# Token rows gathered one product earlier, and the second matrix's blocks in the order 0, 2, 1, 3, in an attention and mixture-of-experts kernel

## The chip, the cores and the metric

One core of a Trainium2 chip runs the whole kernel. The metric is device time in microseconds, from start to end of one execution. Five engines work side by side, each through its own instructions in order, and wait for each other through semaphores: TensorE (PE, matrix products), VectorE (DVE), ScalarE (ACT), GpSimd (POOL) and SyncE (SP, which here only issues DMA transfers). POOL issues the indirect transfers, which pick or place rows by a list of indices.

## The reference

The input goes through attention (the sum of a downsampled and a local one), a dense gated layer, and then a mixture of experts. Only the last part is touched by the change:

```python
def _moe2_ref(x, w_gate, w_output_gate, w1, w2):
    logits = x @ w_gate                       # x: 2304 x 512, 8 experts
    e_idx = np.argmax(logits, axis=1)
    ...                                       # gate_w and eom: two factors per token
    for e in range(8):
        mask = e_idx == e
        h = np.maximum(x[mask] @ w1[e], 0.0)  # w1[e]: 512 x 1024
        ye = h @ w2[e]                        # w2[e]: 1024 x 512
        out[mask] = gate_w[mask, None] * eom[mask, e, None] * ye
```

Everything is in float32.

## The kernel before, in words

Attention, the dense layer and the routing fill the first 500 us. Then the experts are worked through in eight ranks, sorted by the number of their tokens. Rank r has room for `CAPS[r]` tokens: 352, 336, 320, 304, 288, 288, 272, 384, so each has three blocks of up to 128 tokens (`NBLK[r]` is 3).

Precision: each float32 operand is split into a rounded part (hi) and the remainder (lo), and each product is the sum of three matmuls: hi by hi (L425), hi by lo of the tokens (L426), lo of the weights by hi (L427), one triple for each 128 x 128 piece of weights. A matrix of an expert comes as four blocks of 128 x 1024 floats (512 KB). `ew_load` (L757) has SP load a block into one of four `raw` buffers, and `ew_split` (L771) makes ACT write its hi (L775) and then DVE or POOL its lo (L777), after which the raw buffer is free. Past rank 0, blocks 0 and 2 have their lo from POOL, and blocks 1 and 3 from DVE. The tiles are W0 to W3 (hi) and W4 to W7 (lo) for the first matrix, W8 to W11 and W12 to W15 for the second: the lo of block 2 of the second matrix is W14, that of block 1 is W13.

The loop at L1111 runs over r = 0 to 6. One turn of it is two stages on PE:

- The second product of rank r: for each of four slices of columns (`dc`) `gb_step` (L827) runs 8 triples, f = 0 to 7, of which the triples of f = 2i and 2i + 1 read block i of the second matrix. After slice dc follow `x_prep`, which transposes block dc of the rows of rank r + 1 (L750) and splits them (ACT and DVE, L754), the split of block dc of the first matrix of rank r + 1, and the load of block dc of its second matrix.
- The first product of rank r + 1: for i = 0 to 3 the split of block i of the second matrix, then `ga_pair` (L806), which makes h[2i] and h[2i+1] (8 triples; ACT writes the hi, DVE the lo, both L803), then `o_step` (L857), which transposes a block of the results of rank r; DVE scales it (`orow`, L850) and POOL scatters it to the output (L851). Last comes the load of block i of the first matrix of rank r + 2, into the raw buffer that the split at this i has freed.

At i = 0, behind the split of block 0, stands `x_gather(r + 2)`: three indirect transfers on POOL (L732), one per block of rows, into `xr`, which has four buffers. In turn r = 0, at i = 1, `overflow_tables` puts some 25 small instructions on DVE.

In this loop the order of every engine is the order in which the program is written. `by_width` (L645) puts each group of products into one of three arms by the true number of tokens, so the streamed width is at times below `CAPS[r]`.

Of the kernel before, what the change touches and what calls it, by code (L numbers as in the profile page):

```python
# [22 lines left out]
NT, DM, DF, E = 2304, 512, 1024, 8  # L23
# [12 lines left out]
NBLK = [-(-c // P) for c in CAPS]  # L36
NBM = max(NBLK)
CMAX = max(CAPS)
CUTS = (0, 16, 48)
NEG = -1e30  # L40
OOB = 1.0e6
RING = 2 * G
# [7 lines left out]
def attention_moe_kernel(ctx: ExitStack, tc: tile.TileContext, q, k, vw_in, v4_in, w1, w2, w3, w_out,  # L50
# [15 lines left out]
    def mt(shape, dt, name, tag=None, bufs=None):  # L66
        return main.tile(shape, dt, name=name, tag=tag or name, bufs=bufs)
# [15 lines left out]
    for j in range(4):  # L83
        nc.gpsimd.iota(ci[32 * j:32 * j + 32, 0:32], pattern=[[1, 32]], base=0, channel_multiplier=-1)
    nc.vector.tensor_copy(cj[:, 0:32], ci[:, 0:32])
    nc.vector.tensor_scalar(cj[:, 32:64], cj[:, 0:32], 0.0, NEG, op0=ALU.is_lt, op1=ALU.mult)
    nc.vector.tensor_scalar(cj[:, 64:96], cj[:, 0:32], 6.0, NEG, op0=ALU.is_gt, op1=ALU.mult)
    nc.vector.tensor_tensor(
        mask, cj[:, 32:64].unsqueeze(1).to_broadcast([P, 6, 32]),
        cj[:, 64:96].unsqueeze(1).to_broadcast([P, 6, 32]), op=ALU.add)  # L90
    nc.vector.memset(mask[0:32, 0, 0:3], NEG)
    nc.vector.memset(mask[96:128, 5, 27:32], NEG)
    eps4 = mt([P, 1], F32, "eps4")
# [49 lines left out]
    def w_tile(n, shape):  # L143
        return mt(shape, F32R, f"W{n}")
# [500 lines left out]
    def by_width(r, C, products):  # L645
# [3 lines left out]
        def arm(a, b):  # L649
            if b - a == 1:  # L650
                products(C - CUTS[a])
                return
            m = (a + b) // 2
            with tc.If(rt["n"][r] > C - CUTS[m]) as cond:
                arm(a, m)
            with cond.Else():
                arm(m, b)

        arm(0, len(CUTS))

    def reg_of(r):
        if r not in rt["reg"]:
            rt["reg"][r] = nc.sync.value_load(rt["ei"][0:1, r:r + 1], min_val=0, max_val=E - 1)
        return rt["reg"][r]
# [51 lines left out]
        pe[0] = next((i for i in reversed(nc.cur_bb.bb.instructions) if i.engine == mybir.EngineType.PE), None)  # L716
        return res

    def x_gather(r, half=None):
        C = CAPS[r]  # L720
        d = rt.setdefault("xr", {})
        for b in range(NBLK[r]):
            n = min(P, C - P * b)
            if (r, b) not in d:
                d[r, b] = bp.tile([P, DM], F32, name="xr", tag="xr", bufs=4)
            dst, src = d[r, b][0:n], yd
            if half == 0:
                dst, src = dst[:, 0:DM // 2], yd.rearrange("n (t d) -> (n t) d", t=2)
            elif half == 1:
                dst, src = dst[:, DM // 2:DM], yh  # L730
            idx = rt["g2"][0:n, b:b + 1] if half == 0 else rt["gi"][0:n, r, b:b + 1]
            ins = nc.gpsimd.indirect_dma_start(out=dst, out_offset=None, in_=src,  # L732
                                               in_offset=bass.IndirectOffsetOnAxis(ap=idx, axis=0))
        return ins

    def x_prep(r, b, k0=0, k1=KD):
        C = CAPS[r]
        if r not in xT:
            if r == 0:
                even = [mt([P, KD, CMAX], F32R, "xT", tag=tag) for tag in ("xh", "xl")]  # L740
                xT.update({i: even for i in range(0, E, 2)})
            else:
                odd = mt([P, 2, KD, CMAX], F32R, "xT", tag="wc")
                xT.update({i: (odd[:, 0], odd[:, 1]) for i in range(1, E, 2)})
        n = min(P, C - P * b)
        t = rt["xr"][r, b]
        ps = at_psum()
        pv = ps[:, 0:512].rearrange("p (k n) -> p k n", k=KD)
        for kk in range(k0, k1):
            nc.tensor.transpose(pv[:, kk, 0:n], t[0:n, P * kk:P * kk + P], ident[0:n, 0:n])  # L750
        c = slice(P * b, P * b + n)
        x = pv[:, k0:k1, 0:n]
        hi, lo = xT[r][0][:, k0:k1, c], xT[r][1][:, k0:k1, c]
        return nc.scalar.copy(out=hi, in_=x), nc.vector.tensor_tensor(lo, x, hi.bitcast(F32), op=ALU.subtract)  # L754
# [3 lines left out]
    def ew_load(r, m, i, t=None):  # L758
        reg = reg_of(r)
        if t is None:  # L760
            t = bp.tile([P, 1024], F32, name="raw", tag="raw", bufs=4)
        if m == 0:
            ins = nc.sync.dma_start(out=t,
                              in_=e_w1[bass.ds(reg, 1), P * i:P * i + P, :].rearrange("o p n -> p (o n)"))
        else:
            ins = nc.sync.dma_start(out=t,
                              in_=e_w2[bass.ds(reg, 1), P * i:P * i + P, :].rearrange("o p n -> p (o n)"))
        raws[r, m, i] = t
        return ins

    def ew_split(r, m, i):  # L771
        t = raws.pop((r, m, i))
        hi = w_tile(8 * m + i, [P, 1024])
        lo = w_tile(8 * m + 4 + i, [P, 1024])
        nc.scalar.copy(out=hi, in_=t)  # L775
        eng = nc.vector if i % 2 != (r == 0 and m == 1) or (r == 0 and m == 0) else nc.gpsimd
        ins = eng.tensor_tensor(lo, t, hi.bitcast(F32), op=ALU.subtract)  # L777
        ew[r, m, i] = (hi, lo)
        return ins
# [32 lines left out]
    def ga_pair(r, f0):  # L812
        C = CAPS[r]
        for f in (f0, f0 + 1):
            gp[f] = psb.tile([P, 512], F32, name="g1", tag="g1", bufs=4)

        def products(n):
            hi, lo = ew[r, 0, f0 // 2]
            for f in (f0, f0 + 1):
                for kk in range(KD):  # L820
                    c = slice(256 * kk + P * (f % 2), 256 * kk + P * (f % 2) + P)
                    mm3n(gp[f], n, C, hi[:, c], lo[:, c], xT[r][0][:, kk], xT[r][1][:, kk], kk == 0, kk == KD - 1)

        by_width(r, C, products)
        return [ga_out(r, f) for f in (f0, f0 + 1)]
# [3 lines left out]
    def gb_step(r, dc):  # L829
        C = CAPS[r]  # L830
        if dc == 0:
            if not oT:
                oT["all"] = mt([P, 2, KD, CMAX], F32, "oT", tag="xr")
            oT[r] = oT["all"][:, r % 2]
        ps = ps2.tile([P, 512], F32, name="g2", tag="g2")

        def products(n):
            for f in range(KF):
                hi, lo = ew[r, 1, f // 2]
                c = slice(512 * (f % 2) + P * dc, 512 * (f % 2) + P * dc + P)  # L840
                t = h2[r, f]
                mm3n(ps, n, C, hi[:, c], lo[:, c], t[:, 0], t[:, 1], f == 0, f == KF - 1)

        by_width(r, C, products)
        nc.scalar.copy(out=oT[r][:, dc, 0:C], in_=ps[:, 0:C])
# [11 lines left out]
    def o_step(r, b):  # L857
        n = min(P, CAPS[r] - P * b)
        ps = at_psum()
        for dc in range(KD):  # L860
            nc.tensor.transpose(ps[0:n, P * dc:P * dc + P], oT[r][:, dc, P * b:P * b + n], ident)
        o_out(r, b, ps)

    def gb_rows(r, b):
        ps = ps2.tile([P, 512], F32, name="g2", tag="g2")
        c = slice(P * b, P * b + P)
        for f in range(KF):
            hi, lo = (w[:, 512 * (f % 2):512 * (f % 2) + 512] for w in ew[r, 1, f // 2])
            t = h2[r, f]
            mm3(ps, t[:, 0, c], t[:, 1, c], hi, lo, f == 0, f == KF - 1)  # L870
        o_out(r, b, ps)
# [192 lines left out]
    for i in range(2):  # L1064
        ew_load(0, 0, i)
    ordered(g2_step, NG - 1, 0, 0)
    rows = x_gather(0, 1)
    behind(rows, ew_load(0, 0, 2))
    behind(rows, ew_load(0, 1, 0, early[:, 0]))
# [6 lines left out]
    with tc.issue_after(store.ins):  # L1076
        ew_load(0, 1, 1, early[:, 1])
    rows = x_gather(0, 0)
    behind(rows, ew_load(0, 0, 3))
    last = ordered(x_prep, 0, NBLK[0] - 1, KD // 2, KD)  # L1080
# [31 lines left out]
    with tc.manual_schedule(engines={et.PE, et.DVE, et.Activation, et.Pool, et.SP}):  # L1112
        for r in range(E - 1):
            for dc in range(KD):
                gb_step(r, dc)
                if dc < NBLK[r + 1]:
                    x_prep(r + 1, dc)
                ew_split(r + 1, 0, dc)
                ew_load(r + 1, 1, dc)
            for i in range(4):  # L1120
                ew_split(r + 1, 1, i)
                if i == 0 and r + 2 < E:
                    x_gather(r + 2)
                ga_pair(r + 1, 2 * i)
                if i < NBLK[r]:
                    o_step(r, i)
                if r + 2 < E:
                    ew_load(r + 2, 0, i)
                if (r, i) == (0, 1):
                    overflow_tables()  # L1130
        for b in range(NBLK[E - 1]):
            gb_rows(E - 1, b)
# [62 lines left out]
```

## Time and profile before

| what | value |
|---|---|
| median of 3 runs | 729.62 us (725.38 to 732.04) |
| the profiled execution | 732.17 us |
| its span, first to last instruction | 730.1 us |
| PE busy | 690.3 us, 95% |
| DVE, ACT, POOL busy | 381.6, 286.1, 332.4 us |
| mean granted TensorE clock | 0.983 of full |

The profile is of one execution. Times in it count from the first instruction. A busy PE row overlaps the next: matmuls are pipelined, and their pace is the distance between the starts of two rows. Where an instruction waited, its row ends with a bracket: the idle time of its engine before it, and what ended that. The executions of the loop are read between 500 and 707 us.

### The profile page before, as it was taken

The numbers are of one execution on the slowest core, as the hardware profiler recorded it, in microseconds if no ns is written. First come the engines' busy times: TensorE is split into PE (matmuls) and PEld (weight loads), VectorE is DVE, ScalarE is ACT, GpSimd is POOL, SyncE is SP. The second block draws the span as 40 slices with busy tenths as digits, with TensorE's granted clock in tenths as the row PEclk, the third lists the DMA queues.
The fourth block names the chain that finished last, engine by engine and source line by source line (L and its number), as shares of the span: only waits on it lengthen the run. The fifth ranks groups of instructions, "written<-read, shape, count | busy, mean of one in ns | idle before, by whom it ended". The sixth has DMA issues, their size and how long they took to land.

```text
span 730.1 us, 14874 instructions
## 1 busy us (share of the span) xinstructions
PE 690.3 (95%) x5710; PEld 659.1 (90%) x5711; DVE 381.6 (52%) x887; ACT 286.1 (39%) x664; POOL 332.4 (46%) x339
## 2 busy tenths in 40 slices
PE   5888999998999999999999999989999999989995
PEld 3787988898999999999999999969999999989994
DVE  8898889853645346253242342563545345345340
ACT  3455525562354136135212221234534545545520
POOL 5976468863474047124002020142636466567431
PEclk9999999998999999999999999989999999999999
DMA  8878545363143124111010100455647456566501
GB/s 325 266 252 275 199 137 193 108 196 119 50 136 110 44 73 119 64 41 45 23 44 1 43 1 30 146 194 173 211 127 235 127 191 216 176 208 231 170 31 42
DMA packets 38287, 98.08 MB, mean 134 GB/s; under 512 B 6019, under 2 KB 12931, under 8 KB 38193
## 3 DMA queue, kind: packets, MB, share of 16 engines
q1 hardware_dynamic: 34768, 86.82, 37.5%
q0 software_dynamic: 3424, 9.93, 3.7%
q8 instruction: 68, 1.11, 0.6%
q14 instruction: 27, 0.21, 0.1%
HBM read 84.93 MB, written 12.29 MB: 133 GB/s over the span
## 4 chain that ended last, share of the span: by engine, by line
PE 52%; issue 18%; POOL 16%; DMA 7%; DVE 6%; ACT 1%; SPq 0%; POOLq 0%; DVEq 0%; ACTq 0%
PE g L419 14%; PE g L421 13%; PE g L420 13%; POOL W L777 6%; POOL out_dram L851 3%; POOL xr L732 2%; DMA v<-in_v_dram 2%; PE at L282 2%; DMA vw<-in_vw_dram 1%; PE g L427 1%; PE at L222 1%; PE g L425 1%; DVE cv L140 1%; PE g L426 1%; PE at L278 1%
## 5 line engine op out<-in xcount | busy, mean ns | idle before, releaser
L419 PE MATMUL g<-xh,W 128*128 128x384 f32 x384 | 131.9, 343 | 0.9 <-ACT a L453 0.9
L421 PE MATMUL g<-xh,W 128*128 128x384 f32 x384 | 129.2, 337 | 0.8 <-POOL W L398 0.7
L420 PE MATMUL g<-xl,W 128*128 128x384 f32 x384 | 129.2, 336 | 0.0
L777 POOL TENSOR_TENSOR W<-raw,W 128x1024 fp32r<-128x1024 f32 x29 | 70.3, 2424 | 78.3 <-ACT W L775 78.3
L458 POOL TENSOR_TENSOR h<-a,h 128x384 fp32r<-128x384 f32 x30 | 30.6, 1020 | 101.6 <-ACT h L456 101.6
L419 PEld LDWEIGHTS g<-xh,W 128*128 128x128 f32 x384 | 72.2, 188 | 2.5 <-ACT a L453 1.2
L421 PEld LDWEIGHTS g<-xh,W 128*128 128x128 f32 x384 | 72.1, 188 | 1.9 <-POOL W L398 1.8
L420 PEld LDWEIGHTS g<-xl,W 128*128 128x128 f32 x384 | 72.2, 188 | 0.1
L427 PE MATMUL g<-h,W 128*128 128x320 f32 (+4 forms) x224 | 66.2, 296 | 3.9 <-POOL W L777 3.9
L425 PE MATMUL g<-h,W 128*128 128x320 f32 (+7 forms) x224 | 68.3, 305 | 1.2 <-ACT xT L754 0.8
L419 PE MATMUL g<-wc,h 128*128 128x272 f32 (+1 forms) x240 | 69.3, 290 | 0.0
L420 PE MATMUL g<-wc,h 128*128 128x272 f32 (+1 forms) x240 | 68.9, 289 | 0.0
L425 PE MATMUL g<-xT,W 128*128 128x288 f32 (+5 forms) x224 | 68.8, 307 | 0.0
L421 PE MATMUL g<-wc,h 128*128 128x272 f32 (+1 forms) x240 | 68.6, 288 | 0.0
L426 PE MATMUL g<-h,W 128*128 128x320 f32 (+4 forms) x224 | 66.1, 295 | 0.8 <-DVE h L803 0.8
L427 PE MATMUL g<-xT,W 128*128 128x320 f32 (+4 forms) x224 | 66.4, 296 | 0.0
L426 PE MATMUL g<-xT,W 128*128 128x320 f32 (+4 forms) x224 | 66.3, 296 | 0.0
L775 ACT CAST W<-raw 128x1024 fp32r<-128x1024 f32 x61 | 63.2, 1048 | 5.5 <-DMA raw<-in_moe_w_dram 5.5
L777 DVE TENSOR_TENSOR W<-raw,W 128x1024 fp32r<-128x1024 f32 x32 | 41.4, 1294 | 38.0 <-ACT W L775 33.2
L454 DVE TENSOR_TENSOR a<-g,a 128x384 f32<-128x384 f32 x48 | 26.6, 554 | 55.0 <-PE g L421 47.0
L803 DVE SCALAR_TENSOR_TENSOR h<-g,h 128x288 fp32r<-128x288 f32 (+6 forms) x64 | 30.5, 486 | 31.0 <-ACT h L803 20.2
L803 ACT ACTIVATE h<-g 128x288 fp32r<-128x288 f32 (+6 forms) x64 | 27.4, 436 | 48.6 <-PE g L427 37.4
(266 smaller groups left out, 1746.6 us busy)
## 6 DMA issues: line engine op xcount, KB each, us to landing
raw<-in_moe_w_dram SPq DMA_DIRECT2D x61, 512.0 KB
f64w<-in_moe_w_dram SPq DMA_DIRECT2D x16, 512.0 KB
f<-in_moe_w_dram SPq DMA_DIRECT2D x16, 512.0 KB
vw<-in_vw_dram SPq DMA_DIRECT2D x16, 384.0 KB
kc<-in_k_dram SPq DMA_DIRECT2D x16, 288.0 KB
qT<-in_q_dram SPq DMA_DIRECT2D x16, 288.0 KB
kz<-in_k_dram SPq DMA_DIRECT2D x32, 144.0 KB
v<-in_v_dram SPq DMA_DIRECT2D x16, 288.0 KB
```

The lines of the kernel that those rows point to most:

```text
L419: nc.tensor.matmul(ps, whi, xhi, start=first, stop=False)
L420: nc.tensor.matmul(ps, whi, xlo, start=False, stop=False)
L421: return nc.tensor.matmul(ps, wlo, xhi, start=False, stop=last)
L425: nc.tensor.matmul(ps[:, 0:w], whi, xhi[:, 0:w], start=first, stop=False)
L426: nc.tensor.matmul(ps[:, 0:n], whi, xlo[:, 0:n], start=False, stop=False)
L427: nc.tensor.matmul(ps[:, 0:n], wlo, xhi[:, 0:n], start=False, stop=last)
L454: nc.vector.tensor_tensor(a, pp[1][:, 0:G], a, op=ALU.mult)
L458: eng.tensor_tensor(lo, a, hi.bitcast(F32), op=ALU.subtract)
L775: nc.scalar.copy(out=hi, in_=t)
L777: ins = eng.tensor_tensor(lo, t, hi.bitcast(F32), op=ALU.subtract)
L803: return nc.scalar.activation(out=t[:, 0, 0:C], in_=ps[:, 0:C], func=AF.Relu), nc.vector.scalar_tensor_tensor(t[:, 1, 0:C], ps[:, 0:C], 0. ...
L851: ins = nc.gpsimd.indirect_dma_start(out=out, out_offset=bass.IndirectOffsetOnAxis(ap=rt["si"][0:n, r, b:b + 1], axis=0), in_=t[0:n], in_o ...
```

## The change

The gather is called block by block. The three blocks of the rows of rank r + 2 are now gathered in the second product of rank r, one behind each of the slices 0, 1 and 2, in place of all three in the first product of rank r + 1. The second matrix of rank r + 1 is loaded, and later split, in the order of blocks 0, 2, 1, 3. Which engine makes the lo of a block stays as it was (0 and 2 POOL, 1 and 3 DVE), so the two splits of POOL now come one after the other, and then the two of DVE.

```diff
+W2ORDER = (0, 2, 1, 3)
-    def x_gather(r, half=None):
+    def x_gather(r, half=None, blocks=None):
         C = CAPS[r]
         d = rt.setdefault("xr", {})
-        for b in range(NBLK[r]):
+        for b in range(NBLK[r]) if blocks is None else blocks:
...
                 ew_split(r + 1, 0, dc)
-                ew_load(r + 1, 1, dc)
+                if r + 2 < E and dc < NBLK[r + 2]:
+                    x_gather(r + 2, blocks=(dc,))
+                ew_load(r + 1, 1, W2ORDER[dc])
             for i in range(4):
-                ew_split(r + 1, 1, i)
-                if i == 0 and r + 2 < E:
-                    x_gather(r + 2)
+                ew_split(r + 1, 1, W2ORDER[i])
                 ga_pair(r + 1, 2 * i)
```

The line numbers of the changed kernel are one higher than those before, down to the loop.

On POOL, in turn r = 5, from the split of block 0 of the first matrix to the last scatter. L777 rows are the lo of a block, `xr` rows a gather, `out_0_dram` rows a scatter. Before:

```order
L777 TENSOR_TENSOR W4_10076<-raw_9706,W0_10075 128x1024
L777 TENSOR_TENSOR W6_10254<-raw_9902,W2_10253 128x1024
L777 TENSOR_TENSOR W12_10342<-raw_10079,W8_10341 128x1024
L732 DMA xr_10345<-yd_72,b_gi_5790 128x512
L732 DMA xr_10347<-yd_72,b_gi_5790 128x512
L732 DMA xr_10349<-yd_72,b_gi_5790 128x512
L851 DMA out_0_dram<-orow_10447,b_si_5791 2304x512
L851 DMA out_0_dram<-orow_10554,b_si_5791 2304x512
L777 TENSOR_TENSOR W14_10562<-raw_10257,W10_10561 128x1024
L851 DMA out_0_dram<-orow_10652,b_si_5791 2304x512
```

The same stretch of POOL in the changed kernel:

```order
L778 TENSOR_TENSOR W4_10076<-raw_9706,W0_10075 128x1024
L733 DMA xr_10079<-yd_72,b_gi_5790 128x512
L733 DMA xr_10170<-yd_72,b_gi_5790 128x512
L778 TENSOR_TENSOR W6_10258<-raw_9902,W2_10257 128x1024
L733 DMA xr_10261<-yd_72,b_gi_5790 128x512
L778 TENSOR_TENSOR W12_10348<-raw_10081,W8_10347 128x1024
L852 DMA out_0_dram<-orow_10447,b_si_5791 2304x512
L778 TENSOR_TENSOR W14_10464<-raw_10172,W10_10463 128x1024
L852 DMA out_0_dram<-orow_10554,b_si_5791 2304x512
L852 DMA out_0_dram<-orow_10652,b_si_5791 2304x512
```

The gathers have moved from behind W12 to places behind W4 and W6, and W14 from behind the second scatter to behind the first.

On DVE, in the first product of the same turn: L777 rows are the lo of a block, `h` rows the lo of the hidden values, `orow` rows the scaled results. Before:

```order
L850 TENSOR_SCALAR orow_10447<-tr_10442,b_gv_6014 128x512
L777 TENSOR_TENSOR W13_10464<-raw_10168,W9_10463 128x1024
L803 SCALAR_TENSOR_TENSOR h2_10543<-g1_10467,h2_10543 128x272
L803 SCALAR_TENSOR_TENSOR h3_10546<-g1_10468,h3_10546 128x272
L850 TENSOR_SCALAR orow_10554<-tr_10549,b_gv_6014 128x512
L803 SCALAR_TENSOR_TENSOR h4_10641<-g1_10565,h4_10641 128x272
L803 SCALAR_TENSOR_TENSOR h5_10644<-g1_10566,h5_10644 128x272
L850 TENSOR_SCALAR orow_10652<-tr_10647,b_gv_6014 32x512
L777 TENSOR_TENSOR W15_10660<-raw_10339,W11_10659 128x1024
```

In the changed kernel:

```order
L851 TENSOR_SCALAR orow_10447<-tr_10442,b_gv_6014 128x512
L804 SCALAR_TENSOR_TENSOR h2_10543<-g1_10467,h2_10543 128x272
L804 SCALAR_TENSOR_TENSOR h3_10546<-g1_10468,h3_10546 128x272
L851 TENSOR_SCALAR orow_10554<-tr_10549,b_gv_6014 128x512
L778 TENSOR_TENSOR W13_10562<-raw_10263,W9_10561 128x1024
L804 SCALAR_TENSOR_TENSOR h4_10641<-g1_10565,h4_10641 128x272
L804 SCALAR_TENSOR_TENSOR h5_10644<-g1_10566,h5_10644 128x272
L851 TENSOR_SCALAR orow_10652<-tr_10647,b_gv_6014 32x512
L778 TENSOR_TENSOR W15_10660<-raw_10345,W11_10659 128x1024
```

W13 has moved from ahead of h2 to ahead of h4; the rest of DVE's order stands.

## Rows read from the trace of the kernel before

**Rows 1.** The page: busy time, share of the span and instructions of each engine.

```profile
PE 690.3 (95%) x5710; PEld 659.1 (90%) x5711; DVE 381.6 (52%) x887; ACT 286.1 (39%) x664; POOL 332.4 (46%) x339
```

**Rows 2.** Waits of PE, whole span: us in total, times, longest us.

```profile
PE g L427 <- POOL W L777: 3.9, 3, 1.3
PE g L426 <- DVE h L803: 0.8, 1, 0.8
```

**Rows 3.** Timeline of PE: start us, us, instruction, [idle before <-releaser].

```profile
623.04 0.38 PE L427 MATMUL g<-h,W 128*128 128x240 f32 x1 [1.29 <-POOL W L777]
...
649.23 0.38 PE L427 MATMUL g<-h,W 128*128 128x240 f32 x1 [1.32 <-POOL W L777]
...
673.13 0.30 PE L425 MATMUL g<-h,W 128*128 128x272 f32 x1
...
674.60 0.27 PE L426 MATMUL g<-h,W 128*128 128x224 f32 x1
676.18 0.37 PE L427 MATMUL g<-h,W 128*128 128x224 f32 x1 [1.31 <-POOL W L777]
```

**Rows 4.** Timeline of POOL, turn r = 5.

```profile
659.54 2.40 POOL L777 TENSOR_TENSOR W<-raw,W 128x1024 fp32r<-128x1024 f32 x1 [4.47 <-ACT W L775]
663.58 2.50 POOL L777 TENSOR_TENSOR W<-raw,W 128x1024 fp32r<-128x1024 f32 x1 [1.64 <-ACT W L775]
666.23 1.80 POOL L732 DMA_INDIRECT xr<-yd,b_gi  x1
...
669.61 0.95 POOL L732 DMA_INDIRECT xr<-yd,b_gi  x1 [0.30 <-issue]
670.87 1.02 POOL L851 DMA_INDIRECT out_dram<-orow,b_si  x1 [0.30 <-issue]
672.19 1.54 POOL L851 DMA_INDIRECT out_dram<-orow,b_si  x1 [0.30 <-issue]
673.74 2.39 POOL L777 TENSOR_TENSOR W<-raw,W 128x1024 fp32r<-128x1024 f32 x1
```

**Rows 5.** Timeline of ACT, turn r = 5: the hi of the second and third block split.

```profile
664.21 1.04 ACT L775 CAST W<-raw 128x1024 fp32r<-128x1024 f32 x1
...
667.35 1.04 ACT L775 CAST W<-raw 128x1024 fp32r<-128x1024 f32 x1
```

**Rows 6.** Timeline of DVE, turn r = 5.

```profile
664.71 0.74 DVE L850 TENSOR_SCALAR orow<-tr,b_gv 128x512 f32<-128x512 f32 x1
665.37 1.79 DVE L777 TENSOR_TENSOR W<-raw,W 128x1024 fp32r<-128x1024 f32 x1
...
667.85 0.74 DVE L850 TENSOR_SCALAR orow<-tr,b_gv 128x512 f32<-128x512 f32 x1
...
670.62 0.44 DVE L803 SCALAR_TENSOR_TENSOR h<-g,h 128x272 fp32r<-128x272 f32 x1 [0.91 <-issue]
670.98 0.73 DVE L850 TENSOR_SCALAR orow<-tr,b_gv 32x512 f32<-32x512 f32 x1
671.64 1.20 DVE L777 TENSOR_TENSOR W<-raw,W 128x1024 fp32r<-128x1024 f32 x1
...
674.62 0.44 DVE L803 SCALAR_TENSOR_TENSOR h<-g,h 128x272 fp32r<-128x272 f32 x1 [1.09 <-ACT h L803]
```

**Rows 7.** Timeline of DVE, turn r = 0, in the overflow tables.

```profile
525.43 0.17 DVE L889 TENSOR_SCALAR b_b<-i 128x18 f32<-128x18 f32 x1
...
525.98 3.03 DVE L893 TENSOR_SCALAR b_b<-b_b 128x18 f32<-128x18 f32 x1
```

**Rows 8.** Timeline of POOL, turn r = 0: W14.

```profile
526.53 2.44 POOL L777 TENSOR_TENSOR W<-raw,W 128x1024 fp32r<-128x1024 f32 x1
```

**Rows 9.** Timeline of SP, turn r = 5: the four loads of the second matrix.

```profile
655.10 9.08 SPq L766 DMA_DIRECT2D raw<-in_moe_w_dram  x4
```

**Rows 10.** Two stretches (second, first product), engines' busy us, PEclk, DMA share, GB/s.

```profile
647.00:661.01 14.01, 11.93 (x103) 11.39 (x102) 3.66 (x6) 6.00 (x11) 6.91 (x4) 1.00 0.52 169
661.01:673.13 12.12, 12.12 (x110) 12.08 (x109) 8.62 (x13) 7.79 (x13) 9.11 (x7) 1.00 0.70 228
```

## The prediction

> **What bounds the kernel now.** I read the busy times first. PE is busy for 690.3 of 730.1 us [rows 1], so only what PE waits for counts. Next I read the waits of PE. In the loop over the ranks its largest named wait is for a lo of weights made by POOL: 3.9 us in three waits, 1.3 us the longest [rows 2]. The timeline of PE puts them at 623.04, 649.23 and 676.18, so in the turns r = 3, 4 and 5, of 1.29, 1.32 and 1.31 us, always on the last matmul of a triple of f = 4, which reads the lo of block 2, W14 [rows 3]. The turns before have no such wait; their products are wider and give POOL more time.
>
> The timeline of POOL tells why W14 is late [rows 4]. In turn 5 POOL makes W12 until 666.08, then three gathers from 666.23 to 670.56, two scatters until 673.73, and only then W14, from 673.74 to 676.13. PE had started its triple of f = 4 and would have gone on at 674.71 (the start of the matmul before, 674.60, and a pace of 0.11 us): W14 is 1.42 us late. Its hi was written long before: in turn 5 ACT casts block 2 at 667.35, until 668.39 [rows 5]. So POOL's queue is late, not data.
>
> **What the change does to W14.** It takes about 4.3 us of gathers out of POOL's queue ahead of W14 (666.23 to 670.56 [rows 4]), and one scatter. I lay turn 5 out anew, with PE as it is now. W12 ends at 666.08 as before. The first scatter needs the first `orow`, which DVE ends at 665.45 [rows 6], and takes 1.02 [rows 4]: until 667.1. Block 2 now has the cast that block 1 had, which ends at 665.25 [rows 5]. So W14 runs from 667.1 to 669.5, 5.2 us before PE wants it. What a slow scatter (1.54 [rows 4]) or a late W12 could add does not use that up. The three waits go: **3.92 us**.
>
> **Where the gathers go.** Their six places a turn cost POOL nothing that ends on PE. The first two fall into the 4.47 us in which POOL idles before W6 [rows 4]; at 0.95 and 0.30 us between them they take 2.5, at the stretched 1.80 each 4.2. The third falls between the end of W6 (661.94) and the start of W12 (663.58), 1.64 us: 0.95 fits, 1.80 makes W12 about 0.6 us late, which comes off the 5.2 us of W14. A gather needs a free `xr` buffer; there are four, and each gather stands behind the transposes that free its own. The rows come a stage sooner than now, and no wait for them stands in this loop. Price: 0, and at worst 0.6 us of slack.
>
> The gathers' transfers now share the DMA engines with loads of the second matrix instead of the first. The second product is the emptier stage: 0.52 of the engines at 169 GB/s, against 0.70 at 228 [rows 10]. In turn 5 the four loads begin at 655.10 [rows 9], and the second block must be there at 664.21 [rows 5]: 9.1 us. Two loads are 1.05 MB, 4.6 us at 228 GB/s; three gathers of 128 rows of 2 KB are 0.79 MB, 3.4 us. Even with all gathers ahead of them the loads have 1.1 us left. Estimated cost: 0.
>
> **The new order of blocks.** Loads and splits keep their distance, since both use the same order. The raw buffer that W14 now frees at i = 1 was freed by DVE at 667.16 [rows 6], and is now at 669.5: the load into it is issued 2.3 us later, but its block is cast only in the next second product, over 10 us on. The load that waited for W14 until 676.13 is issued when W13 ends. Cost: 0.
>
> On DVE, W13 leaves the place ahead of h2 and stands ahead of h4. Its cast is now the third one, which ends at 668.39 [rows 5]; the second `orow` ends at 668.59 [rows 6]. There it meets POOL's W14, until 669.5. What such a meeting costs is in the rows: W13 takes 1.79 us from 665.37, of which POOL's W12 covers the part until 666.08, while W15, which meets no split of POOL, takes 1.20 [rows 4, 6]. The excess, 0.59 us, is about the overlap of 0.71. So W13 ends between 669.8 (no hindrance) and 670.7 (it waits for W14). I take 670.7, by that row. Then h4 and h5 (0.44 each) until 671.6, the third `orow` until 672.3, W15 until 673.5, h6 until 674.0. h7 starts as now at 674.62, because ACT's hi sets it, and ends at 675.06 [rows 6]. PE wants these from its start of this product, 673.13 [rows 3], at 0.113 us a matmul (13 of them to 674.60): h6 by the 20th, 675.3; W15 by the 21st, 675.4; h7 by the 23rd, 675.6. The margins are 1.3, 1.9 and 0.5 us. So W13's move costs 0, but the next thing to be late is this chain of DVE.
>
> The Trainium skill, SBUF — State Buffer, section on who interferes with whom, says that a VectorE instruction with two SBUF inputs and a GpSimd instruction that reads SBUF exclude one another, and that the one issued first holds the port to its end. By that rule W13 waits for W14 in full. The trace agrees (1.79 beside 1.20 us [rows 6]). By it the change brings two such instructions closer together; the sum stays at 3.9 us as long as DVE's margins hold, and is the first rival below where they don't.
>
> **Turn r = 0.** PE also waits once for an h of DVE, 0.8 us [rows 2]. There a DVE instruction of the overflow tables takes 3.03 us, where one of the same size takes 0.17 [rows 7]; it ends at 529.01, and POOL's W14 runs from 526.53 to 528.97 [rows 8]. With two gathers' and more work gone ahead of it, W14 will be over before 525.98. That gives DVE back 2.86 us, and W13, which now stands behind the tables, takes 1.2 of it. The chain to h6 is then some 1.6 us earlier, and the wait goes: 0.8 us. Bounds: if the long instruction stays for another reason, W13 makes the chain 1.2 us later and PE waits up to 2.0, a loss of 1.2. I take the gain of 0.8, since both ends of the long instruction fit W14.
>
> **Sum.** 3.92 + 0.8 = 4.7 us. Against the profiled execution, 732.17 us, that is 727.5. The median of the three runs is 729.62, 2.55 below the profiled one; the same 4.7 us below it is 724.9, my forecast: 0.6% faster. A measurement of this kernel tells about 1% (7.3 us) from no change, so this is "within 1%".
>
> **Rivals.**
>
> 1. DVE's chain takes the place of W14: no change. For it speaks the thin margin of h7, 0.5 us. The bound: POOL's second and third scatter (1.0 us each) each go first and hold DVE up as W14 does. W13 then ends at 671.7, the third `orow` at 673.3, W15 at 675.5, h6 at 675.95, h7 at 676.4, and PE waits 0.8 us. In all six turns r = 0 to 5 that is 4.8 us and eats the gain: about 729.7. Against it: before, a scatter that met W15 was itself stretched (1.54 us beside 1.02 [rows 4]), and W15 was not (1.20 [rows 6]). Half of it would give 727.
> 2. Slower: gathers and loads of the second matrix get in each other's way. The point from which it decides is 4.5 us of delay of the second block (9.1 less 4.6); the gathers' own bytes are worth 3.4. If each turn's cast came 2 us late beyond that and ACT, which then holds h2 and h3 back, passed it on to PE in six turns, that is 12 us less 4.7: 737. Against it: the second product leaves nearly half of the DMA time free [rows 10].
> 3. The change doesn't reach PE: W14 is still late, because its scatter in front waits for something else. It would have to wait 5.2 us more than now. The time would stay at 729.6.
> 4. More than I count: an earlier W14 also frees raw buffers and the loads behind them sooner, and PE's small waits elsewhere in these turns go as well. Their whole is some 2 us: 722.5.
>
> **How the numbers follow.** Forecast (3.9 to 4.7 us less) 0.62, rival 1 in part or whole 0.18, rival 2 0.08, rival 3 0.04, rival 4 0.08. The forecast's own range is 722 to 728, as medians of three runs that spread from 725.38 to 732.04 move by about 3 us. To hold 8 in 10 I reach over rival 1 and a part of rival 4, from 720.5 to 731. Faster by over 1% (below 722.3) needs rival 4 or a low set of runs: 0.14. Slower by over 1% (above 736.9) is rival 2: 0.07. Within 1%: 0.79.
>
> **What would show it.** In the profile after: no wait of PE for W L777; W14 in turn 5 over some 5 us before its triple; POOL's gathers behind W4 and W6; W13 of about 2 us where it meets W14; no 3.03 us in the tables. Wrong would be a wait of PE for DVE's h or W in the turns 3 to 5 (rival 1), or ACT's cast of the second or third block waiting for a DMA (rival 2).

## The result, and the profile after

The changed kernel takes 720.36 us (median of 7 runs, 719.58 to 724.86) against 728.89 us before (7 runs, 725.38 to 732.04). The ratio is 0.9904, with a 95% interval from 0.9875 to 0.9934: about 1.0% faster, between 4.8 and 9.1 us. Timed again later beside the kernel before, it was 722.27 against 728.26 us, ratio 0.9898 (0.9852 to 0.9944). So the sign and the forecast of "within 1%" are right, the forecast of 4.7 us is too small (the loop below gave 7.4), and 720.36 lies just below the range. By the two medians alone it is 8.5 us, 1.2%.

In the profile after, PE is busy for 96% of a span of 717.8 us; the row is laid out as [rows 1]:

```profile
PE 686.0 (96%) x5710; PEld 657.0 (92%) x5711; DVE 377.1 (53%) x887; ACT 286.8 (40%) x664; POOL 334.7 (47%) x339
```

The two profiled spans differ by 12.3 us, more than the medians do, so a part of that belongs to single executions. The loop over the ranks can be cut out: it runs from the first matmul of the second product of rank 0 to the first one of rank 7. On the timeline of PE in the changed kernel these are:

```profile
493.38 0.32 PE L426 MATMUL g<-h,W 128*128 128x352 f32 x1
...
674.67 0.35 PE L426 MATMUL g<-xT,W 128*128 128x384 f32 x1
```

That is 181.29 us. In the kernel before, the same two are at 498.72 and 687.40, 188.68 us. The loop gave **7.4 us**; 5.3 us of the difference of the spans lie ahead of it, where both programs are the same. In three executions of the changed kernel the loop took 181.29, 181.31 and 181.31 us, while its start moved from 493.38 to 500.72. The loop is the sharper measure, and all kernels below are compared by it.

One cause of the 5.3 us is to be seen. In the kernel before, PE waited 2.3 us for a transfer of the attention (`vw`, L282) between 165 and 175 us, and the granted clock then fell for some microseconds. By stretch, with the columns of [rows 10], before and after:

```profile
165.00:180.00 15.00, 12.72 (x99) 11.94 (x99) 4.47 (x14) 2.37 (x6) 5.63 (x7) 0.77 0.44 137
```

```profile
165.00:180.00 15.00, 14.89 (x124) 14.06 (x123) 6.20 (x31) 3.06 (x8) 6.09 (x8) 1.00 0.41 130
```

0.77 of full clock against 1.00, and 99 matmuls against 124. Nothing of the change is near, and a third execution of the changed kernel waits there too, 2.1 us at the longest: this belongs to single executions.

Inside the loop, PE has no wait at all after the change. The list of its waits over the whole span (columns as in [rows 2]) has only lines of earlier and of transitional stages; its longest are

```profile
PE g L348 <- POOL qz L159: 5.8, 1, 5.8
PE g L420 <- DVE wc L385: 3.7, 3, 2.9
```

and both rows of [rows 2] are gone. POOL in turn 5 answers to [rows 4]:

```profile
645.70 1.00 POOL L733 DMA_INDIRECT xr<-yd,b_gi  x1 [0.16 <-issue]
647.01 1.31 POOL L733 DMA_INDIRECT xr<-yd,b_gi  x1 [0.30 <-issue]
648.99 2.40 POOL L778 TENSOR_TENSOR W<-raw,W 128x1024 fp32r<-128x1024 f32 x1 [0.68 <-ACT W L776]
651.54 0.96 POOL L733 DMA_INDIRECT xr<-yd,b_gi  x1
653.04 2.51 POOL L778 TENSOR_TENSOR W<-raw,W 128x1024 fp32r<-128x1024 f32 x1 [0.54 <-ACT W L776]
655.69 1.02 POOL L852 DMA_INDIRECT out_dram<-orow,b_si  x1
656.73 2.43 POOL L778 TENSOR_TENSOR W<-raw,W 128x1024 fp32r<-128x1024 f32 x1
```

The gathers fill gaps that POOL had; W6 (648.99) and W12 (653.04) still wait for their cast by ACT, not for a gather. The last row is W14: it ends at 659.16. PE's triple that reads it comes at

```profile
664.17 0.27 PE L428 MATMUL g<-h,W 128*128 128x224 f32 x1
```

so W14 is 5.0 us early where it was 1.42 us late. DVE in the same turn answers to [rows 6]:

```profile
657.96 2.30 DVE L778 TENSOR_TENSOR W<-raw,W 128x1024 fp32r<-128x1024 f32 x1
660.18 0.78 DVE L804 SCALAR_TENSOR_TENSOR h<-g,h 128x272 fp32r<-128x272 f32 x2
660.88 0.73 DVE L851 TENSOR_SCALAR orow<-tr,b_gv 32x512 f32<-32x512 f32 x1
661.54 1.20 DVE L778 TENSOR_TENSOR W<-raw,W 128x1024 fp32r<-128x1024 f32 x1
662.67 0.99 DVE L804 SCALAR_TENSOR_TENSOR h<-g,h 128x272 fp32r<-128x272 f32 x2
```

W13 takes 2.30 us, since it meets W14 (until 659.16, and 1.10 us on). h7 ends at 663.66; PE wants it 22 matmuls of 0.113 us after 662.59, at 665.1.

Where the 7.4 us lie, by the length of the single products (start to start of PE's rows):

| product | before, us | after, us | difference |
|---|---|---|---|
| second of rank 1 (turn 0's wait for h) | 16.67 | 15.54 | 1.13 |
| second of rank 4 (W14) | 13.85 | 12.30 | 1.55 |
| second of rank 5 (W14 and one short wait) | 14.85 | 12.28 | 2.57 |
| second of rank 6 (W14 and one short wait) | 14.27 | 12.08 | 2.19 |
| the other nine | 129.04 | 129.09 | -0.05 |

### The profile page after: what moved, and what is told of

Its sections match the earlier page's. It is cut to its first block, busy times and chain, and to the rows that moved or that the text cites. A ratio compares the mean times of both kernels' runs of the same rounds, so it can differ in the third digit from the quotient of the medians.

```text
span 717.8 us, 14882 instructions
## 1 busy us (share of the span) xinstructions
PE 686.0 (96%) x5710; PEld 657.0 (92%) x5711; DVE 377.1 (53%) x887; ACT 286.8 (40%) x664; POOL 334.7 (47%) x339
## 4 chain that ended last, share of the span: by engine, by line
PE 69%; DVE 9%; POOL 7%; issue 6%; DMA 5%; ACT 2%; SPq 0%; POOLq 0%; DVEq 0%; ACTq 0%
PE g L420 13%; PE g L422 13%; PE g L421 13%; PE g L426 8%; PE g L428 7%; PE g L427 7%; DVE cv L141 2%; DVE cv L140 2%; DVE wf L142 1%; PE tr L751 1%; PE at L283 1%; DMA v<-in_v_dram 1%; DMA kc<-in_k_dram 1%; PE tr L862 1%; POOL out_dram L852 1%
## 5 line engine op out<-in xcount | busy, mean ns | idle before, releaser
L852 POOL DMA_INDIRECT out_dram<-orow,b_si x24 | 33.2, 1384 | 37.5 <-DVE orow L851 36.0
```

Source lines behind the costliest of these rows:

```text
L852: ins = nc.gpsimd.indirect_dma_start(out=out, out_offset=bass.IndirectOffsetOnAxis(ap=rt["si"][0:n, r, b:b + 1], axis=0), in_=t[0:n], in_o ...
```

## The experiments

The loop is cut out as above. "None" means no wait of PE over 0.3 us in it, "without cause" that no semaphore explains the wait.

| kernel | loop, us | waits of PE in the loop |
|---|---|---|
| before, two executions | 188.68, 187.86 | W14 three times, h in turn 0, one or two short ones |
| changed, three executions | 181.29, 181.31, 181.31 | none |
| gathers alone, two executions | 183.72, 183.57 | h in turn 0, one or more short ones |
| order alone | 188.60 | h four times, W13 in turn 0, two of 1.2 without cause |
| changed, late loads | 183.13 | one of 1.2 without cause |
| changed, extra transfers | 187.29 | two without cause, 2.7 and 1.3 |
| the same, one arm | 192.42 (wider products) | none |
| changed, late h6 | 190.78 | h6 three times, by construction |

### The kernel before again

No edit; a second execution.

> The kernel before, looked at in a second execution, to see which of its waits belong to it and which to one execution. In the first profile the loop takes 188.7 us from the start of the second product of rank 0 to the start of the first product of rank 7; the changed kernel takes 181.3. Theory: the three waits for W14 (1.3 us each, turns 3 to 5), the wait for an h of DVE in turn 0 (0.8) and two short waits of PE behind slice 1 of the second products of ranks 5 and 6 (0.76 and 0.46 us) all come again, and the loop takes 188.7 within 0.5. Rival: the two short waits are chance; they are gone or elsewhere, and the loop takes about 187. What lies before the loop may differ by several us.

```profile
PE g L427 <- POOL W L777: 3.9, 3, 1.3
PE g L426 <- DVE h L803: 0.8, 1, 0.8
PE g L425 <- PE tr L750: 0.6, 1, 0.6
```

The list of PE's waits in this execution, from 490 us on. The waits for W14 and for h are the same to a tenth. Of the two short ones, that of rank 5 came again (0.6 in place of 0.76 us), that of rank 6 did not, and the loop is 0.8 us shorter. So the named waits belong to the kernel; the short ones come at like places, and not always. Their releaser is named as ACT in one execution and PE itself in the other, so the name given is not to be relied on.

### The gathers alone, the order alone

The first leaves the order of blocks as it was, the second the gathers:

```diff
-W2ORDER = (0, 2, 1, 3)
+W2ORDER = (0, 1, 2, 3)
```

> Only the gathers are moved; the blocks keep the order 0, 1, 2, 3. Theory (the gathers in POOL's queue made W14 late): W14 stands behind two scatters, and in turn 5 ends at 672 on the scale of the profile before, 2.7 us ahead of PE; the three waits for W14 are gone and the two short ones with them. In turn 0 W14 still meets the overflow tables of DVE, so that a tiny DVE instruction of about 3 us and PE's wait of some 0.8 to 1.1 us stay. Loop 182.4 us, time about 1 us over the changed kernel. Rival (the place behind the second scatter is what made it late): the waits for W14 stay at 2 us or more in sum, loop 186 or more.

```diff
-                if r + 2 < E and dc < NBLK[r + 2]:
-                    x_gather(r + 2, blocks=(dc,))
                 ew_load(r + 1, 1, W2ORDER[dc])
             for i in range(4):
                 ew_split(r + 1, 1, W2ORDER[i])
+                if i == 0 and r + 2 < E:
+                    x_gather(r + 2)
```

> Only the order of the blocks is changed to 0, 2, 1, 3; the gathers stay behind the first split of the second matrix. Theory: W14 then stands behind the gathers and one scatter, and ends at 674.3 in turn 5, 0.4 us ahead of PE, and by 0.6 and 0.7 us in turns 3 and 4: the waits for W14 go, just so. In turn 0 W14 still meets the tables (about 525.3 to 527.7), and W13 now stands behind them, so PE's wait there stays near 1 us. Loop 182.4 to 183.5 us. Rival (only the gathers matter): waits for W14 stay at 2 us or more in sum, loop 185 or more.

Gathers alone: 719.23 us against 727.39, ratio 0.9878 (0.9845 to 0.9910), loop 183.72. Order alone: 726.58 us against the same 727.39, ratio 0.9997 (0.9970 to 1.0024), loop 188.60. **The gathers carry the change; the order alone is worth nothing.**

PE's waits in the loop with the gathers alone:

```profile
PE g L426 <- ACT xT L755: 1.1, 1, 1.1
PE g L427 <- DVE h L804: 0.8, 1, 0.8
```

The waits for W14 are gone, as expected. The loop is 1.3 us longer than expected (182.4), since a short wait of 1.1 us stands in rank 4, where I had expected none. That in turn 0 stays, as expected: there POOL makes W14 from 519.50 to 521.92, and a tiny instruction of the tables on DVE takes 2.92 us, from 519.03 to 521.95.

With the order alone the waits for POOL go too, and that much of the expectation holds, but others take their place:

```profile
PE g L427 <- DVE h L804: 2.0, 4, 1.2
PE g L426 <- ACT xT L755: 1.2, 1, 1.2
PE g L426 <- issue: 1.2, 1, 1.2
PE g L428 <- DVE W L778: 0.9, 1, 0.9
```

This I had not expected, though a part of it is what the prediction held as its first rival. The timelines of POOL and of DVE in turn 5 show how:

```profile
665.08 1.02 POOL L852 DMA_INDIRECT out_dram<-orow,b_si  x1 [0.30 <-issue]
666.11 2.42 POOL L778 TENSOR_TENSOR W<-raw,W 128x1024 fp32r<-128x1024 f32 x1
```

```profile
665.88 3.75 DVE L778 TENSOR_TENSOR W<-raw,W 128x1024 fp32r<-128x1024 f32 x1
669.55 0.78 DVE L804 SCALAR_TENSOR_TENSOR h<-g,h 128x272 fp32r<-128x272 f32 x2
```

W14 is behind the gathers still, and now meets W15, the last split of DVE. W15 takes 3.75 us in place of 1.20 [rows 6]: it begins in POOL's scatter, is held up through all of W14 (until 668.53), and ends 1.10 us later. h6 and h7 are behind it, and PE waits for them, 0.8 us in the turns 3 to 5 together. The Trainium skill, SBUF — State Buffer, section on who interferes with whom, has these two instructions exclude one another for their whole length, the one that is issued first ahead. 3.75 us is 2.42 and 1.20 with a wait behind the scatter, which agrees in length; that W14, which began 0.23 us after W15, went ahead of it does not. The same happens in turn 0, where W14 meets the first of the tables' instructions,

```profile
518.82 3.18 DVE L883 TENSOR_TENSOR b_cm<-b_rank,i 128x64 f32<-128x64 f32 x1
```

and W13, now behind the tables, is late as well: 0.92 us for W13 and 1.17 for h. In the changed kernel W14 runs from 516.60 to 519.00, before the tables begin, and the instruction of 3.03 us [rows 7] is one of 0.18:

```profile
520.91 0.18 DVE L894 TENSOR_SCALAR b_b<-b_b 128x18 f32<-128x18 f32 x1
```

So the order adds to the gathers what turn 0 loses, 1.0 us. Without them it takes away as much as it gives: the 3.9 us of waits for W14 are gone, and by the idle times 0.8 us for h in the turns 3 to 5, 1.3 us in turn 0 (0.92 and 1.17 in place of 0.83) and 1.1 us of short waits (1.17 and 1.16 in place of 0.76 and 0.46) come in their place. The rest is the slower pace of PE behind a wait. The short waits are those of one execution each.

### The short waits: late loads, or after-effects

Before, W14 held back raw buffers, so that two loads of the next first matrix were issued some 3 us into the second product. This kernel does the same with W14 early:

```diff
-                gb_step(r, dc)
+                done = gb_step(r, dc)
...
+                if dc == 0 and r in (5, 6):
+                    for i in (2, 3):
+                        behind(done, ew_load(r + 1, 0, i))
...
-                if r + 2 < E:
+                if r + 2 < E and not (r in (4, 5) and i >= 2):
                     ew_load(r + 2, 0, i)
```

> The changed kernel, but in turns 4 and 5 the loads of blocks 2 and 3 of the first matrix are issued only when slice 0 of the next second product has left PSUM, some 3 us into it, which is when the kernel before issued them; W14 stays early. Theory A (the two short waits of PE behind slice 1 in ranks 5 and 6 come from loads that a late W14 held back): they come again, 0.4 to 1.1 us each, with no wait for W14; loop 182.3 to 183.3. Theory B (they are an after-effect of PE's wait for W14): no wait, loop 181.3 within 0.3.

Neither came. The loop took 183.13 us, as theory A had it, but by one wait in another place, in the first product of rank 5:

```profile
643.15 0.37 PE L426 MATMUL g<-xT,W 128*128 128x288 f32 x1 [1.20 <-DVE orow L851]
```

Late loads of the same two blocks do not bring the waits of ranks 5 and 6 back, so that they alone caused these is not shown. The run did not set up the case of before either, as the packets that bring instructions (below) show: before, the packet of rank 5 started at 652.43, behind late loads issued at 649.20 and 649.77; here it started at 648.43, ahead of the loads (649.40 and 649.97), and in rank 6 at 672.72, ahead of those from 673.77 on. The other question, whether such a wait is the after-effect of PE's own wait, was put by making h6 late:

```diff
+                if i == 3 and r in (3, 4, 5):
+                    pad = mt([P, G], F32, "pad", tag="t2k", bufs=3)
+                    for _ in range(8):
+                        nc.vector.memset(pad, 0.0)
```

> The changed kernel with eight fillings of a scratch tile on DVE (about 3 us) between W15 and h6 in turns 3, 4 and 5, which makes PE wait for h6 there, 1 to 1.6 us each, without holding back any load. Theory B (the short waits behind slice 1 in ranks 5 and 6 are an after-effect of PE's wait a slice earlier): waits of 0.4 to 1.1 us follow there. Theory F: a wait of PE gives its instructions time to come, and none follows beyond the one or two that every arrangement has. Loop 185 to 186 by F, about 187 by B.

The eight fillings took 4.05 us, not 3, and PE waited 2.19, 2.13 and 2.27 us; the list of its waits in the loop has nothing else:

```profile
PE g L427 <- DVE h L804: 6.6, 3, 2.3
```

No wait behind slice 1 followed, so theory B falls. The loop was 190.78 us, longer than either theory said: the waits were larger than meant, and behind the first of them the clock fell.

```profile
619.00:622.00 3.00, 0.81 (x8) 0.62 (x7) 2.38 (x7) 0.00 (x0) 0.00 (x0) 1.00 0.79 300
622.00:624.00 2.00, 2.00 (x12) 2.00 (x13) 0.18 (x1) 0.71 (x2) 0.00 (x0) 0.63 0.02 7
624.00:626.00 2.00, 2.00 (x12) 2.00 (x12) 0.69 (x1) 1.22 (x2) 0.69 (x1) 0.52 0.00 0
626.00:629.00 3.00, 3.00 (x29) 3.00 (x28) 0.41 (x1) 1.43 (x3) 2.70 (x2) 1.00 0.16 26
```

PE waited until 621.88, and in the 4 us after it ran at 0.63 and 0.52 of full clock, near the lower of its two levels (1.2 GHz): 12 matmuls in 2 us, where the stretch at full clock has 29 in 3. That product lost 1.9 us more than the wait itself. Behind the other two waits the clock stayed at 1.00, and the products lost 0.5 and 0.4 us more.

### The short waits: PE's instructions

The queue that brings instructions (q8 on the page) shows single packets, 16 KB each. In eight of the nine of these waits that are longer than 0.4 us, over five kernels, PE went on 2.3 to 2.6 us after the start of a packet; in the ninth, with late loads, after 4.3 us, and there the packet itself was slow (2.5 us). In the changed kernel a packet starts at 641.81 and slice 2 of rank 5, where the kernel before waits, begins at 644.41, 2.6 us later, with no wait. To test whether transfers can bring such waits about, one transfer of 1 MB from memory to memory was put into turns 3 to 6 (its result is not used), once in the changed kernel and once with a single arm for all widths, in which PE skips no instructions:

```diff
+    spare = dram.tile([512, DM], F32, name="spare")
...
+                if dc == 0 and r >= 3:
+                    nc.sync.dma_start(out=spare, in_=yd[0:512])
```

> The changed kernel with one more transfer from memory to memory (1 MB, its result is not used) issued by SP at the start of the second products of ranks 3, 4, 5 and 6. Theory F: waits of PE without a releaser come in most of these four products, 0.5 to 3 us each, while waits for W or h stay below 0.3 us; each ends 2.4 to 3 us after a packet of the instruction queue. Loop 183 to 190. Rival (they have nothing to do with transfers): at most one such wait, loop 181.3 to 182.8.

```diff
-CUTS = (0, 16, 48)
+CUTS = (0,)
```

> The same extra transfers, and the products have one arm only, so that PE runs through its program without skipping two arms of three; the streamed width is then always the full one, and each turn is longer by up to a fifth. Theory F: PE goes through its instructions a third as fast, and the waits without a releaser of the run with the extra transfers are gone or under 0.5 us in sum. Rival (the transfers slow PE's operands or its stores): the waits stay as there.

With three arms PE's waits are in ranks 5 and 6 (on its timeline):

```profile
648.38 0.58 PE L427 MATMUL g<-h,W 128*128 128x288 f32 x1 [2.70 <-issue]
...
676.55 0.27 PE L427 MATMUL g<-h,W 128*128 128x224 f32 x1 [1.31 <-issue]
```

They end 2.5 and 2.3 us after a packet (645.85 and 674.28). They came in two of the four products, where I had expected most. Behind the first the clock fell too, and that product lost 1.8 us more than the wait (columns as in [rows 10]):

```profile
648.40:650.40 2.00, 2.00 (x9) 2.00 (x10) 0.10 (x1) 0.00 (x0) 0.93 (x1) 0.50 0.91 309
```

What held the packet up is to be seen in the share of the 16 DMA engines (last column but one), in the second product of rank 5. First the changed kernel, then the one with the extra transfers:

```profile
638.50:641.50 3.00, 3.00 (x29) 3.00 (x29) 0.52 (x2) 0.70 (x2) 0.46 (x1) 1.00 1.02 417
642.00:644.00 2.00, 2.00 (x20) 2.00 (x20) 0.69 (x1) 1.07 (x2) 0.84 (x1) 1.00 0.00 0
```

```profile
639.50:645.00 5.50, 5.50 (x52) 5.50 (x51) 1.22 (x3) 2.25 (x4) 1.30 (x2) 1.00 1.07 431
646.00:647.50 1.50, 0.00 (x0) 0.00 (x0) 0.92 (x2) 1.24 (x2) 1.35 (x2) 1.00 0.00 0
```

In both the packet starts as the engines run empty of data, 3.6 us into the product in the one (641.81) and 6.6 us in the other (645.85), where PE had stood still since 645.68. In the kernel before, the late loads filled the engines around its packet (652.43):

```profile
650.50:653.00 2.50, 2.50 (x25) 2.50 (x24) 0.69 (x1) 1.93 (x3) 0.30 (x1) 1.00 0.92 318
```

With one arm there is no wait of PE in the loop at all, with the same extra transfers. The instruction queue in the stretch from 600 to 690 us, three arms and then one (packets, MB, share of 16 engines):

```profile
q8 instruction: 17, 0.28, 1.2%
```

```profile
q8 instruction: 6, 0.10, 0.4%
```

So these waits are PE waiting for its next instructions, as far as one execution of each shows: they come with transfers that hold the packet up, and go when PE runs through its program a third as fast. The one arm also makes the products up to 1.9 us longer, which this run cannot take apart from the fewer instructions. The Trainium skill, Runtime: NRT & Kernel Launch, section on instruction fetch, says that a taken branch to instructions that have not been fetched stops the engine until they are; the 2.70 us with the skipped arms and none without them agree with it.

### The changed kernel again, and beside the gathers alone

> The changed kernel in a second execution. Its first profile has no wait of PE in the loop (181.3 us). In the profiles of four other arrangements of the loop PE has one or two waits of 0.6 to 1.5 us that no semaphore explains, at places that differ, each ending about 2.7 us after a packet of the queue that brings instructions. Theory F (these are PE waiting for its next instructions; they come when a packet is held up): the changed kernel can have one too, 0 to 1.5 us in sum; no named wait over 0.3 us; loop 181.3 to 182.8. Rival (the gathers' new place does away with them): none, loop 181.3 within 0.2.

The loop took 181.31 us with no wait over 0.3 us. Then both were timed together, in five rounds:

> Only the gathers moved, timed beside the changed kernel on one chip, to see what the order of the blocks adds. By the two profiles it adds 1.0 us in turn 0 (the overflow tables) and the absence of one wait for instructions of 1.4 us: 2.4 us, 0.3%. Theory: this kernel is 1 to 2.5 us slower than the changed one, and its loop again takes 183.7 us with the wait for an h of DVE in turn 0 (0.8) and the one wait without a releaser in rank 4. Rival (the order adds nothing that lasts): the two are within 0.5 us.

> The changed kernel, timed beside the one with the gathers alone. Theory: loop 181.3 us as in both earlier profiles, no wait of PE over 0.3 us in it, time 1 to 2.5 us below the kernel with the gathers alone. Rival: within 0.5 us of it.

Gathers alone: 721.22 us (ratio 0.9892, 0.9849 to 0.9936), loop 183.57, again with the wait of 0.8 us in turn 0, and with three products in ranks 4 and 5 longer by 0.2, 0.7 and 0.4 us, in place of one by 1.3. Changed: 722.27 us (0.9898, 0.9852 to 0.9944), loop 181.31. By the profiles the order is worth 2.3 us in the loop, of which 1.0 is turn 0 and the rest short waits, which differ between executions; by the measured times the two can't be told apart (the gathers alone are even 1.1 us lower), because what lies ahead of the loop moves by more. The theory's 1 to 2.5 us of the total are not shown.

## Why the prediction was right, and where not

- **What bounds the kernel: right.** PE's waits were all that counted, and they went: of 188.7 us in the loop, 7.4.
- **W14 in POOL's queue: right, to the number.** Predicted 5.2 us ahead of PE in turn 5, measured 5.0. With the gathers alone the waits go, and with the order alone too: the gathers and the second scatter together made W14 late, and taking either from ahead of it is enough. What sets the two halves apart is what else they bring.
- **The size of these waits: a little small.** I took the three idle times, 3.92 us [rows 2]. By the pace of the rows around them each cost 0.15 us more (1.45, 1.48, 1.47, in sum 4.4): the matmul after a wait starts slowly.
- **Gathers at no cost: right.** POOL's W6 and W12 wait for ACT as before, and no cast of ACT in the loop waited for a load. Two slips in the text of it changed nothing: a turn has three places for gathers, not six, and a third gather of 1.80 us with the 0.30 before it would make W12 0.5 us late, not 0.6 (it took 0.96).
- **W13 behind W14: right.** 2.30 us in place of an estimated 2.1 (668.59 to 670.7), and hidden. The margin that I feared, h7's 0.5 us, was 1.4, as ACT's hi came sooner (0.20 us behind the start of PE's product, 1.06 before; what held it up there is not shown).
- **Turn 0: right mechanism, mis-sized.** The tables' long instruction was W14's doing, as it follows W14 through four arrangements (3.03, 2.92, 3.18 and 0.18 us). I took 0.8 us, the product became 1.13 shorter.
- **The step that failed** is the sum, where it left PE's short waits out. Only rival 4 has them, as PE's "small waits elsewhere in these turns", with "some 2 us" for it all and a chance of 0.08. The two in ranks 5 and 6 were 1.10 and 0.63 us by the rows' pace, and all of that went: 7.4 is 4.4, 1.13 and 1.73, plus 0.1 of small change. In the second execution of before they were 0.9. So rival 4 is what happened (its 722.5 is 2.4 us below the forecast, where its words say some 2), with its mechanism only half right: these are waits for instructions, which other transfers hold up. That the early loads did away with them fits the DMA share around the packets, but is argued; the run with late loads did not set the case up.
- **Rival 1** did not happen here. With the order alone its mechanism is there, DVE's chain held up behind W14, but it is small: 0.8 us in the turns 3 to 5, where the bound had 0.8 in each of six turns. That the gain is gone there (188.60 us) is as much turn 0 and the short waits.
- **The median** is 8.5 us lower where the loop gives 6.6 to 7.4. The rest is within the interval (4.8 to 9.1), and the loop starts between 492.3 and 500.7 us in the profiles of these kernels, whose program ahead of it is the same. That "within 1%" holds is a near thing: 1.0% by the ratio, with an interval from 0.7 to 1.25%, 1.2% by the medians, and 720.36 is below the 722.3 that the prediction gave as its lower end.

## What to carry to other kernels

When an engine's queue makes a product late, look for work in that queue that nobody waits for yet, and move it a stage earlier into gaps that the engine has; here three gathers a turn cost nothing in their new place. When two splits are put closer together in time on VectorE and GpSimd, lay out where they meet: it costs nothing ahead of a margin (W13) and 0.2 to 0.4 us a turn ahead of the last thing that PE needs (W15). Short waits with an unlikely releaser are worth a row in the sum, as they can go, or come, with any change of the traffic.

## What the runs showed of the hardware

- PE waited 0.5 to 2.7 us for instructions in a loop with branches over unused arms, and went on 2.3 to 2.6 us after the start of a packet of its instruction queue (4.3 where the packet was slow). With 1 MB of extra transfers the packet of rank 5 started 6.6 us into the product in place of 3.6, as the DMA engines ran empty.
- After a wait of PE of 2.2 us the granted clock was 0.63, then 0.52 for the next 4 us, and after one of 2.7 us it was 0.50; after waits of 1.3 us for W14 it stayed at 1.00, and after two others of 2.1 and 2.3 us too.
- A scatter or gather of POOL that starts while VectorE splits a block takes 1.5 to 1.8 us in place of 1.0 [rows 4], ending 0.9 us after the split.
- A split of VectorE that begins in a scatter behind which a split of POOL stands waits for both: 3.6 to 3.75 us in place of 1.20, in the turns 3 to 5 with the order alone.
